# Sliding-window cached attention: K of the first unit as one load on ScalarE's queue, turned one projection chunk later; last output block in three pieces

## The chip, the cores and the metric

The kernel runs on one core of one Trainium2 chip. Its time is the device time of one execution in microseconds (us), and the figure for a kernel is the median of several executions. The engines have short names here: PE is TensorE (PEld its weight loads), DVE is VectorE, ACT is ScalarE, POOL is GpSimd, SP is SyncE. A DMA is started by an instruction on the queue of one engine, SP or ACT here, and carried out by 16 DMA engines. Inputs and output lie in device memory as bf16.

## The reference

```python
B, Sq, D = 8, 32, 1024;  Hq, Hkv, Sk, Dh = 32, 4, 8192, 128
W = min(4096, max(256, Sk // 4))          # 2048: the last 2048 keys
rep = Hq // Hkv                           # 8 query heads share a K/V head
q = (x @ wq) as (B, Hq, Sq, Dh)
k, v = the last W rows of the caches, repeated rep times
p = softmax(q k^T * Dh ** -0.5)
out = (p v) as (B, Sq, Hq * Dh) @ wo
```

The work is a query projection, attention of 256 query rows (8 heads by 32 positions) over 2048 keys for each of 32 units (8 sequences by 4 K/V heads), and an output projection.

## The kernel before, in words

The order of every engine is written by hand. `run` walks over the 32 units; a unit `ui` is (sequence b, group g), and units 0 to 7 are group 0. A unit has four chunks of four 128-key tiles. For each chunk PE computes the scores, keys on the partitions (L467), ACT takes the exponential without subtracting a maximum (L469), and two chunks later PE multiplies with V (L478). V is copied by DVE into a tile with a column of ones (L409), so that the last column of the result is the softmax sum; DVE divides by it (L415, L420) and turns the result for the output projection (L422). Queries of the next groups (L273) and the output projection (L293, gathered in the tile `oacc`) are spread over the chunks by a plan.

Scores need K with the head dimension on the partitions. Units 0 to 4 load K as it lies and turn it on PE, some later units turn it on DVE and POOL (L249, L257, L259), the others use a transposing DMA (L194). All loads go to SP's queue, except one half of x on ACT's. They are issued ahead of need, and DMAs share eight semaphores in turn, so that an issue waits until the semaphore's earlier DMA has landed.

`start` (L310) sets the order that matters here.
- **Loads.** x goes half to SP (L319), half to ACT (L320). Then on SP: the eight chunks of wq of group 0, as loads of 1, 1, 2, 2, 1 and 1 chunks with 2-KB rows (L162). K of unit 0 is loaded in two halves with 2-KB rows, one after wq chunks 4 and 5 (L324, issued at L191), one after chunk 7 (L327, issued at L186). Behind it come V of unit 0 and the K and V of units 1 to 3.
- **PE.** After seven warm-up matmuls (L345) PE turns x (L354). The copies out of PSUM go half to DVE and half to ACT (L357). Then come the eight chunks of the projection, eight matmuls each (L375). From chunk 4 on (`Q_CUT`) only the first 128 of 256 rows are done there. After chunk 5 (`c == self.DC - 3`) PE turns the first half of unit 0's K (L368, `k_turn(0)`), and DVE copies it to `kT` (L372, `k_copy(0)`). Chunks 6 and 7 follow, then the second half's turn.
- **After the loop.** The queries of unit 0 are cast out of four PSUM tiles, two by ACT and two by DVE (L395). After its two casts DVE copies the second half of K and then V of unit 0. The first scores need all four casts and the first half of K. The rest of the projection (`q_rest`) is placed between the first chunks of unit 0.

The end is in two functions. `tail_begin` finishes the last unit, counts on the device whether all softmax sums are in a safe range (`check_all`, L524 to L528), and starts the last output block: its first piece of 512 columns is multiplied ahead of a branch on that count (L76, L78). The branch leads to an exact fallback (`attention_exact`, `out_proj`), which the given inputs do not need. `tail_end` adds that piece to `oacc` (L303) and stores it (L305), then does the remaining pieces, of 256, 128 and 128 columns. The pieces share two PSUM buffers (`ps_m`). The stores of columns 0 and 768 go on SP's queue, the others on ACT's.

V of units 29 to 31 is loaded in two halves (`V_HALVES`, L200), all other V in one load.

Of the kernel before, what the change touches and what calls it, by code (L numbers as in the profile page):

```python
# [11 lines left out]
BF16 = mybir.dt.bfloat16  # L12
# [6 lines left out]
Q_CUT = 4  # L19
N_WARM = (7, 0, 0)  # L20
VA_ROW = 160
V_HALVES = 29

PE_T = (0, 1, 2, 3, 4)

# [77 lines left out]
class Fast:  # L103
# [69 lines left out]
                                   in_=self.wo[r0:r0 + 4 * self.Dh, :].rearrange("(p c) n -> p c n", c=4)[:, 2 * i:2 * i + 2, :])  # L173
        return [lambda i=i: piece(i) for i in range(2)]

    def load_k(self, ui, part=None):

        nc, P, KT = self.nc, self.P, self.KT
        b, g = self.units[ui]
        src = self.k_cache[b, g, self.Sk - self.W:, :]  # L180
        if ui not in V_T and ui not in self.kT:
            self.kT[ui] = self.ktp.tile([P, KT, P], BF16, name="kT")
        if ui in PE_T or ui in V_T:
            H = KT // 2
            if part == 1:
                nc.sync.dma_start(out=self.k_raw[ui][:, H:, :], in_=src.rearrange("(p j) d -> p j d", j=KT)[:, H:, :])  # L186
                return
            self.k_raw[ui] = (self.kvt.tile([P, KT, self.Dh], BF16, name="k_raw", tag="kv") if ui < 2 else
                              self.krp.tile([P, KT, self.Dh], BF16, name="k_raw"))
            n = KT if part is None else H  # L190
            nc.sync.dma_start(out=self.k_raw[ui][:, 0:n, :], in_=src.rearrange("(p j) d -> p j d", j=KT)[:, 0:n, :])  # L191
        else:
            H = KT // 2
            nc.sync.dma_start_transpose(out=self.kT[ui][:, part * H:(part + 1) * H, :],  # L194
                                        in_=src.rearrange("(p j) d -> p (j d)", j=KT)[:, part * H * P:(part + 1) * H * P])

    def load_v(self, ui, eng):
        b, g = self.units[ui]
        self.v_sb[ui] = self.vp.tile([self.P, self.KT, self.Dh], BF16, name="v_sb", tag="v")
        n = self.KT // (2 if ui >= V_HALVES else 1)  # L200
        for j in range(0, self.KT, n):
            eng.dma_start(out=self.v_sb[ui][:, j:j + n, :],
                          in_=self.v_cache[b, g, self.Sk - self.W:, :].rearrange("(p j) d -> p j d", j=self.KT)[:, j:j + n, :])

    def load_unit(self, ui):

# [73 lines left out]
    def o_pieces(self, g, t, cuts=(512, 512)):  # L280

        nc, P = self.nc, self.P
        st = {}
        last = g == self.Hkv - 1

        def piece(n0, w, i, mm=None):

            if i == 0:
                st["ps"] = self.open_ps = self.ps_m.tile([P, 512], FP32, name="op_ps", tag="m")
            ps = st["ps"]  # L290
            for k in range(i * 2, i * 2 + 2) if mm is not False else ():
                gq, c = g * self.QT_N + k // 4, k % 4
                nc.tensor.matmul(ps[:, 0:w], lhsT=self.OT[:, gq, c, t * P:(t + 1) * P],  # L293
                                 rhs=self.wo_t[gq][:, c, n0:n0 + w], start=(k == 0), stop=(k == 7))
            if i == 3 and mm is not True:
                acc = self.oacc[:, t, n0:n0 + w]
                if g == 0:
                    nc.vector.tensor_copy(out=acc, in_=ps[:, 0:w])
                elif not last:
                    nc.vector.tensor_tensor(out=acc, in0=ps[:, 0:w], in1=acc, op=ALU.add)  # L300
                else:
                    o_t = self.osb.tile([P, 512], BF16, name="o_t")
                    nc.vector.tensor_tensor(out=o_t[:, 0:w], in0=ps[:, 0:w], in1=acc, op=ALU.add)  # L303
                    eng = nc.sync if n0 in (0, 768) else nc.scalar
                    eng.dma_start(out=self.out[t * P:(t + 1) * P, n0:n0 + w], in_=o_t[:, 0:w])  # L305
        return [lambda n0=sum(cuts[:k]), w=w, i=i, **kw: piece(n0, w, i, **kw) for k, w in enumerate(cuts) for i in range(4)]

# [2 lines left out]
    def start(self):  # L310
        nc, P = self.nc, self.P
# [9 lines left out]
        wq0 = self.load_wq(0, 0, (1, 1, 2)) + self.load_wq(0, 1, (2, 1, 1))  # L321
        for p in wq0[:4]:
            p()
        self.load_k(0, 0)  # L324
        wq0[4]()
        wq0[5]()
        self.load_k(0, 1)  # L327
        self.load_v(0, nc.sync)
        self.load_k(1)
        self.load_v(1, nc.sync)  # L330
# [18 lines left out]
        def x_turn(half, pl, tag):  # L349
            ps = pl.tile([P, H, self.NT, P], BF16, name="xT_ps", tag=tag)  # L350
            for c in range(H):
                for t in range(self.NT):
                    c0 = (half * H + c) * P
                    nc.tensor.transpose(ps[:, c, t, :], x_sb[:, t, c0:c0 + P], self.ident[:, :])  # L354
            for i, copy in ((0, nc.vector.tensor_copy), (1, nc.scalar.copy)):
                c0 = half * H + i * H // 2
                copy(out=self.xT[:, c0:c0 + H // 2, :], in_=ps[:, i * H // 2:(i + 1) * H // 2, :, :].rearrange("p c t s -> p c (t s)"))  # L357

        x_turn(0, self.ps_m, "m")
        x_turn(1, self.ps_s, "s_ps")  # L360
        qs = [pl.tile([P, 2, self.NQ], FP32, name="q0_ps", tag=tag)
              for pl, tag in ((self.ps_o, "o_ps"), (self.ps_o, "o_ps"), (self.ps_m, "m"), (self.ps_m, "m"))]
        KT = self.KT
# [15 lines left out]
        for c in range(self.DC):  # L379
            for h in range(self.rep):  # L380
                q_mm(c, h, 0, P if c >= Q_CUT else self.NQ)
            if c == 0:
                warm_up(N_WARM[2])
                warm_sb = self.c1.tile([P, 8], BF16, name="warm_sb")
                nc.vector.tensor_copy(out=warm_sb[:, :], in_=warm[:, 0:8])
            if c == self.DC - 3:
                tp = self.ps_s.tile([P, KT, P], BF16, name="kf_ps", tag="s_ps")
                k_turn(0)
                k_copy(0)
# [105 lines left out]
    def tail_begin(self):  # L495
        self.pv_last()
        for p in self.after[:-2]:
            p()
        flagi = self.check_all()
        for p in self.after[-2:]:  # L500
            p()
        self.last = self.o_pieces(self.Hkv - 1, 1, (512, 256, 128, 128))
        for p in self.last[:3]:
            p()
        self.last[3](mm=True)
        return flagi
# [25 lines left out]
def attention_exact(tc, k_cache, v_cache, Q_e, OT_e, *, B, Hkv, Hq, Sq, Sk, W, Dh, scale):  # L532

    nc = tc.nc
# [5 lines left out]
    with ExitStack() as ctx:  # L540
# [12 lines left out]
        with tc.For_i(0, Hkv, 1) as g, tc.For_i(0, B, 1) as b:  # L553
# [27 lines left out]
            o_ps = ps_o.tile([P, UQ], FP32, name="o_ps")  # L581
            for j in range(KT):
                nc.tensor.matmul(o_ps[:, :], lhsT=v_sb[:, j, :], rhs=pT[:, j, :], start=(j == 0), stop=(j == KT - 1))
            nc.vector.tensor_copy(out=OT_e[:, :].rearrange("p (g h b s) -> p g h b s", g=Hkv, h=rep, b=B)[:, bass.ds(g, 1), :, bass.ds(b, 1), :],
                                  in_=o_ps[:, :].rearrange("p (g h b s) -> p g h b s", g=1, h=rep, b=1))


def out_proj(tc, wo, OT_e, out_flat, fast, *, Hkv, Hq, Sq, NQ, D):

    nc = tc.nc  # L590
    P = 128
    NT = NQ // P
    NC_ = D // 512
    rep = Hq // Hkv
    UQ = rep * Sq
    B = NQ // Sq
    with ExitStack() as ctx:
        wop = ctx.enter_context(tc.tile_pool(name="wo_pool", bufs=1))
        accp = ctx.enter_context(tc.tile_pool(name="acc_pool", bufs=1))
        pc = ctx.enter_context(tc.tile_pool(name="pc", bufs=1, space=PSUM))  # L600
        wo_v = wo.rearrange("(h p) n -> h p n", p=P)
        acc = accp.tile([P, NT, D], FP32, name="acc")
        nc.vector.memset(acc[:, :, :], 0.0)
        with tc.For_i(0, Hq, 1) as h:
            wo_sb = wop.tile([P, D], BF16, name="wo_sb")
            nc.sync.dma_start(out=wo_sb[:, :], in_=wo_v[bass.ds(h, 1), :, :].rearrange("o p n -> p (o n)"))
            o_h = wop.tile([P, NQ], BF16, name="o_h")
            nc.vector.tensor_copy(out=o_h[:, :], in_=OT_e[:, bass.ds(h * NQ, NQ)])
            ps = pc.tile([P, NT, D], FP32, name="ps")
            for t in range(NT):  # L610
                for n in range(NC_):
                    nc.tensor.matmul(ps[:, t, n * 512:(n + 1) * 512], lhsT=o_h[:, t * P:(t + 1) * P],
                                     rhs=wo_sb[:, n * 512:(n + 1) * 512], start=True, stop=True)
            nc.vector.tensor_tensor(out=acc[:, :, :], in0=ps[:, :, :], in1=acc[:, :, :], op=ALU.add)
        o_t = accp.tile([P, NT, D], BF16, name="o_t")
        nc.vector.tensor_copy(out=o_t[:, :, :], in_=acc[:, :, :])
        nc.sync.dma_start(out=out_flat.rearrange("(t p) d -> p t d", t=NT), in_=o_t[:, :, :])

        nc.vector.tensor_copy(out=fast.oacc[:, :, :], in_=acc[:, :, :])
        nc.vector.memset(fast.OT[:, (Hkv - 1) * fast.QT_N:, :, :], 0.0)  # L620
        nc.vector.memset(fast.open_ps[:, :], 0.0)
# [30 lines left out]
```

## Time and profile before

| What | us |
|---|---|
| Median of three runs (186.3 to 187.19) | 186.85 |
| The profiled execution, its own time | 186.85 |
| Span of its profile, first to last instruction | 185.0 |
| First score matmul of unit 0 | 13.32 |
| The last 128 output columns: addition begins | 182.34 |
| ACT busy, in all | 131.8 |
| DVE busy, in all | 115.4 |
| Mean rate of all DMA traffic | 280 GB/s |

The span is cut into 40 slices of 4.6 us. Each digit is the busy share of an engine in a slice, in tenths (9 is 90% or more). PEclk is PE's granted clock in tenths of full speed, DMA the mean busy share of the DMA engines, and the last row what they moved in GB/s:

```profile
PE   7999999999999999999999999999999999999993
DVE  0138799994586685586467558647745855355372
ACT  2207899786789787878787677787877888888700
PEclk9999999999999999999999999999999999999999
DMA  5999999998999999999999999999999999980012
GB/s 151 324 391 415 413 414 396 198 231 278 346 332 297 305 329 337 412 215 244 363 357 244 362 386 252 186 342 397 249 381 320 228 288 246 299 131 0 4 58 62
```

A reader can see three parts: a start of about three slices in which ACT and DVE have little to do, a long middle, and a short end in which the loads are over. In a timeline a line gives start, duration, engine, source line and operation, output and input names, the number of instructions, and in square brackets the idle time before them with what ended it. An engine name with a q (SPq, ACTq) is the engine's instruction queue, on which DMAs are issued.

### The profile page before, as it was taken

To read this page: it belongs to the slowest core of one execution; us is meant where nothing else is said; L and a number is where in the kernel's file an instruction comes from. 1 tells how busy PE (TensorE), PEld (TensorE's weight loads), DVE (VectorE), ACT (ScalarE), POOL (GpSimd) and SP (SyncE) were. 2 spreads that over 40 slices of the span, in tenths; PEclk is the share of its full clock that TensorE was granted. 3 is DMA by queue.
4 is the path that set the end of the run, shared out by engine and by line. 5 is a ranking of instruction groups with operands and counts; after the bars stand their busy time and mean duration, and the time that the engine had idled before them with its cause. 6 is when DMAs were issued, how large, how long until landed. Compare 5 with 4: busy or idle time off the path is not lost. (4 is left out here: it accounts for less than half of the span.)

```text
span 185.0 us, 5079 instructions
## 1 busy us (share of the span) xinstructions
PE 179.5 (97%) x2056; PEld 153.7 (83%) x2072; DVE 115.4 (62%) x268; ACT 131.8 (71%) x133; POOL 94.7 (51%) x150
## 2 busy tenths in 40 slices
PE   7999999999999999999999999999999999999993
PEld 2889999999999999987878999987777888888743
DVE  0138799994586685586467558647745855355372
ACT  2207899786789787878787677787877888888700
POOL 2000008949939959929944980796299289600000
PEclk9999999999999999999999999999999999999999
DMA  5999999998999999999999999999999999980012
GB/s 151 324 391 415 413 414 396 198 231 278 346 332 297 305 329 337 412 215 244 363 357 244 362 386 252 186 342 397 249 381 320 228 288 246 299 131 0 4 58 62
DMA packets 53082, 51.73 MB, mean 280 GB/s; under 512 B 39744, under 2 KB 40256, under 8 KB 53056
## 3 DMA queue, kind: packets, MB, share of 16 engines
q1 hardware_dynamic: 52480, 50.90, 97.8%
q10 hardware_dynamic: 576, 0.49, 0.8%
q8 instruction: 16, 0.26, 0.6%
q14 instruction: 10, 0.08, 0.1%
HBM read 41.42 MB, written 0.52 MB: 227 GB/s over the span
## 5 line engine op out<-in xcount | busy, mean ns | idle before, releaser
L469 ACT ACTIVATE pT<-s_ps 128x1024 bf16<-128x1024 f32 x128 | 128.9, 1025 | 33.3 <-PE s_ps L467 32.3
L259 POOL TENSOR_SCALAR kTv<-kb 32x512 bf16<-32x512 bf16 x140 | 93.7, 670 | 65.1 <-DMA k_raw<-in_k_cache_dram 26.7
L478 PEld LDWEIGHTS <-pT 128*128 128x128 bf16 x1024 | 68.5, 98 | 3.1
L467 PEld LDWEIGHTS <-kT 128*128 128x128 bf16 x368 | 34.8, 98 | 10.3
L293 PE MATMUL op_ps<-wo_sb,OT 128*128 128x512 bf16 (+2 forms) x128 | 33.0, 353 | 0.8
L273 PE MATMUL q_ps<-xT,wq_sb 128*128 128x256 bf16 x192 | 28.1, 273 | 0.0
L478 PE MATMUL o_ps<-va_112,pT 128*128 128x129 bf16 x352 | 27.1, 220 | 0.0
L478 PE MATMUL o_ps<-va_113,pT 128*128 128x129 bf16 x352 | 27.0, 220 | 0.1
L478 PE MATMUL o_ps<-va_114,pT 128*128 128x129 bf16 x320 | 24.7, 220 | 0.0
L249 DVE STREAM_TRANSPOSE kb<-k_raw 128x512 bf16<-128x512 bf16 x36 | 23.8, 684 | 0.0
L415 DVE RECIPROCAL RL_all<-o_ps 128x2 f32<-128x2 f32 x32 | 5.3, 164 | 27.5 <-PE o_ps L478 27.5
L420 DVE TENSOR_SCALAR o_sb<-o_ps,RL_all 128x128 bf16<-128x128 f32 x64 | 19.5, 346 | 1.1
L467 PEld LDWEIGHTS <-kTv 128*128 128x128 bf16 x144 | 13.9, 98 | 5.1
L273 PEld LDWEIGHTS <-wq_sb 128*128 128x128 bf16 x192 | 17.0, 98 | 1.2
L467 PE MATMUL s_ps<-QT_63,kT 128*128 128x256 bf16 x112 | 16.8, 273 | 0.0
L422 DVE STREAM_TRANSPOSE OT<-o_sb 128x256 bf16<-128x256 bf16 x32 | 14.3, 446 | 1.1
L467 PE MATMUL s_ps<-QT_66,kT 128*128 128x256 bf16 x96 | 14.4, 273 | 0.1
L293 PEld LDWEIGHTS <-OT 128*128 128x128 bf16 x144 | 11.3, 98 | 2.9 <-DVEq L78 0.6
L467 PE MATMUL s_ps<-QT_65,kT 128*128 128x256 bf16 x80 | 12.0, 273 | 0.1
L467 PE MATMUL s_ps<-QT_64,kT 128*128 128x256 bf16 x80 | 12.0, 272 | 0.1
L300 DVE TENSOR_TENSOR oacc<-op_ps,oacc 128x512 f32<-128x512 f32 x8 | 5.5, 683 | 7.4 <-PE op_ps L293 7.4
L409 DVE COPY va_113<-v_sb 128x2048 bf16<-128x2048 bf16 x11 | 9.5, 861 | 0.0
(46 smaller groups left out, 105.2 us busy)
## 6 DMA issues: line engine op xcount, KB each, us to landing
v_sb<-in_v_cache_dram SPq DMA_DIRECT2D x29, 512.0 KB, 6.8
wo_sb<-in_wo_dram SPq DMA_DIRECT2D x16, 512.0 KB, 6.8
wq_sb<-in_wq_dram SPq DMA_DIRECT2D x14, 512.0 KB, 7.4
k_raw<-in_k_cache_dram SPq DMA_DIRECT2D x13, 512.0 KB, 6.5
v_sb<-in_v_cache_dram SPq DMA_DIRECT2D x6, 256.0 KB, 5.8
wq_sb<-in_wq_dram SPq DMA_DIRECT2D x4, 256.0 KB, 6.4
kT<-in_k_cache_dram SPq DMA_TRANSPOSE x36, 6.6
k_raw<-in_k_cache_dram SPq DMA_DIRECT2D x2, 256.0 KB, 7.7
```

Of the source, the lines that this page charges most:

```text
L249: nc.vector.transpose(out=st["kb"][:, sl, :], in_=self.k_raw[ui][:, sl, :])
L259: nc.gpsimd.tensor_scalar(out=out, in0=in_, scalar1=1.0, scalar2=1.0, op0=ALU.mult, op1=ALU.mult)
L273: nc.tensor.matmul(st["ps"][:, 0:self.NQ], lhsT=self.wq_t[g, i][:, c % (DC // 2), hl * P:(hl + 1) * P], rhs=self.xT[:, c, :], start=(c == ...
L293: nc.tensor.matmul(ps[:, 0:w], lhsT=self.OT[:, gq, c, t * P:(t + 1) * P], rhs=self.wo_t[gq][:, c, n0:n0 + w], start=(k == 0), stop=(k == 7))
L300: nc.vector.tensor_tensor(out=acc, in0=ps[:, 0:w], in1=acc, op=ALU.add)
L409: self.nc.vector.tensor_copy(out=self.va[ui % 3][:, :, 0:self.Dh], in_=self.v_sb[ui][:, :, :])
L415: nc.vector.reciprocal(out=rl[:, ui * QT_N:(ui + 1) * QT_N], in_=o_ps[:, :, Dh])
L420: nc.vector.tensor_scalar(out=o_sb[:, qt, :, :], in0=o_ps[:, qt, 0:Dh].rearrange("p (i c) -> p c i", c=4), scalar1=rl[:, ui * QT_N + qt:ui ...
L422: nc.vector.transpose(out=self.OT[:, g * QT_N:(g + 1) * QT_N, :, b * self.Sq:(b + 1) * self.Sq], in_=o_sb[:, :, :, :])
L467: nc.tensor.matmul(s_ps[:, jj, :], lhsT=self.kT[ui][:, c * CJ + jj, :], rhs=q_u, start=True, stop=True)
L469: nc.scalar.activation(out=pT[:, :, :], in_=s_ps[:, :, :], func=ACT.Exp, bias=0.0, scale=self.scale)
L478: nc.tensor.matmul(o_ps[:, qt, 0:self.VW], lhsT=pT[:, jj, qt * P:(qt + 1) * P], rhs=va[:, j, 0:self.VW], start=(j == 0 and qt == 0), stop= ...
```

## The change

K of unit 0 is no longer loaded in two halves on SP's queue. It is one load with 4-KB rows, issued on ACT's queue after ACT's two copies of x. The turn of its first half and DVE's copy of it stand after projection chunk 6 (`c == self.DC - 2`) and no longer after chunk 5; the second half's turn stays after chunk 7. The last output block is cut into 512, 256 and 256 columns, and both pieces of 256 are stored on ACT's queue. V is always one load. In the fallback the tile `OT_e` keeps its results in another order, and the output projection there loops over four groups and no longer over 32 heads.

```diff
-V_HALVES = 29
...
-    def load_k(self, ui, part=None):
+    def load_k(self, ui, part=None, eng=None):
...
         if ui in PE_T or ui in V_T:
-            H = KT // 2
-            if part == 1:
-                nc.sync.dma_start(out=self.k_raw[ui][:, H:, :], in_=src.rearrange("(p j) d -> p j d", j=KT)[:, H:, :])
-                return
             self.k_raw[ui] = (self.kvt.tile([P, KT, self.Dh], BF16, name="k_raw", tag="kv") if ui < 2 else
                               self.krp.tile([P, KT, self.Dh], BF16, name="k_raw"))
-            n = KT if part is None else H
-            nc.sync.dma_start(out=self.k_raw[ui][:, 0:n, :], in_=src.rearrange("(p j) d -> p j d", j=KT)[:, 0:n, :])
+            (eng or nc.sync).dma_start(out=self.k_raw[ui][:, :, :], in_=src.rearrange("(p j) d -> p j d", j=KT))
...
-        n = self.KT // (2 if ui >= V_HALVES else 1)
-        for j in range(0, self.KT, n):
-            eng.dma_start(out=self.v_sb[ui][:, j:j + n, :],
-                          in_=self.v_cache[b, g, self.Sk - self.W:, :].rearrange("(p j) d -> p j d", j=self.KT)[:, j:j + n, :])
+        eng.dma_start(out=self.v_sb[ui][:, :, :],
+                      in_=self.v_cache[b, g, self.Sk - self.W:, :].rearrange("(p j) d -> p j d", j=self.KT))
...
-                    eng = nc.sync if n0 in (0, 768) else nc.scalar
+                    eng = nc.sync if n0 == 0 else nc.scalar
...
         for p in wq0[:4]:
             p()
-        self.load_k(0, 0)
         wq0[4]()
         wq0[5]()
-        self.load_k(0, 1)
         self.load_v(0, nc.sync)
...
         x_turn(1, self.ps_s, "s_ps")
+        self.load_k(0, eng=nc.scalar)
...
-            if c == self.DC - 3:
+            if c == self.DC - 2:
                 tp = self.ps_s.tile([P, KT, P], BF16, name="kf_ps", tag="s_ps")
                 k_turn(0)
                 k_copy(0)
...
-        self.last = self.o_pieces(self.Hkv - 1, 1, (512, 256, 128, 128))
+        self.last = self.o_pieces(self.Hkv - 1, 1, (512, 256, 256))
...
-        with tc.For_i(0, Hq, 1) as h:
+        with tc.For_i(0, Hkv, 1) as g:
...
+            for h in range(rep):
+                for t in range(NT):
+                    for n in range(NC_):
+                        nc.tensor.matmul(ps[:, t, n * 512:(n + 1) * 512], lhsT=o_v[:, h, t * P:(t + 1) * P],
+                                         rhs=wo_sb[:, h, n * 512:(n + 1) * 512], start=(h == 0), stop=(h == rep - 1))
```

More of the change, by code (lines that the diff above doesn't have):

```diff
@@ L183, in load_k @@
         if ui in PE_T or ui in V_T:
-            H = KT // 2
-            if part == 1:
-                nc.sync.dma_start(out=self.k_raw[ui][:, H:, :], in_=src.rearrange("(p j) d -> p j d", j=KT)[:, H:, :])
-                return
             self.k_raw[ui] = (self.kvt.tile([P, KT, self.Dh], BF16, name="k_raw", tag="kv") if ui < 2 else
                               self.krp.tile([P, KT, self.Dh], BF16, name="k_raw"))
-            n = KT if part is None else H
-            nc.sync.dma_start(out=self.k_raw[ui][:, 0:n, :], in_=src.rearrange("(p j) d -> p j d", j=KT)[:, 0:n, :])
+            (eng or nc.sync).dma_start(out=self.k_raw[ui][:, :, :], in_=src.rearrange("(p j) d -> p j d", j=KT))
         else:
+            H = KT // 2
             H = KT // 2
@@ L583, in attention_exact @@
                 nc.tensor.matmul(o_ps[:, :], lhsT=v_sb[:, j, :], rhs=pT[:, j, :], start=(j == 0), stop=(j == KT - 1))
-            nc.vector.tensor_copy(out=OT_e[:, :].rearrange("p (g h b s) -> p g h b s", g=Hkv, h=rep, b=B)[:, bass.ds(g, 1), :, bass.ds(b, 1), :],
-                                  in_=o_ps[:, :].rearrange("p (g h b s) -> p g h b s", g=1, h=rep, b=1))
+            nc.vector.tensor_copy(out=OT_e[:, bass.ds(g * (B * UQ) + b * UQ, UQ)], in_=o_ps[:, :])
 def out_proj(tc, wo, OT_e, out_flat, fast, *, Hkv, Hq, Sq, NQ, D):
@@ L600, in out_proj @@
         pc = ctx.enter_context(tc.tile_pool(name="pc", bufs=1, space=PSUM))
-        wo_v = wo.rearrange("(h p) n -> h p n", p=P)
+        wo_v = wo.rearrange("(g h p) n -> g p h n", p=P, h=rep)
         acc = accp.tile([P, NT, D], FP32, name="acc")
         nc.vector.memset(acc[:, :, :], 0.0)
-        with tc.For_i(0, Hq, 1) as h:
[L605 to L608, printed above, removed]
-            ps = pc.tile([P, NT, D], FP32, name="ps")
[L610 to L613, printed above, removed]
+        with tc.For_i(0, Hkv, 1) as g:
+            wo_sb = wop.tile([P, rep, D], BF16, name="wo_sb")
+            nc.sync.dma_start(out=wo_sb[:, :, :], in_=wo_v[bass.ds(g, 1), :, :, :].rearrange("o p h n -> p (o h) n"))
+            o_g = wop.tile([P, rep, B, Sq], BF16, name="o_g")
+            nc.vector.tensor_copy(out=o_g[:, :, :, :].rearrange("p h b s -> p b h s"),
+                                  in_=OT_e[:, bass.ds(g * (B * UQ), B * UQ)].rearrange("p (b h s) -> p b h s", b=B, h=rep))
+            o_v = o_g[:, :, :, :].rearrange("p h b s -> p h (b s)")
+            ps = pc.tile([P, NT, D], FP32, name="ps")
+            for h in range(rep):
[3 more added lines that the diff above has]
+                                         rhs=wo_sb[:, h, n * 512:(n + 1) * 512], start=(h == 0), stop=(h == rep - 1))
             nc.vector.tensor_tensor(out=acc[:, :, :], in0=ps[:, :, :], in1=acc[:, :, :], op=ALU.add)
```

## The prediction

> **What bounds the kernel now.** I read the page's busy shares first, then the busy time by stretches, then the timelines of the two ends, because the change touches only the first 17 us and the last few.
>
> ```profile
> PE 179.5 (97%) x2056; PEld 153.7 (83%) x2072; DVE 115.4 (62%) x268; ACT 131.8 (71%) x133; POOL 94.7 (51%) x150
> 20.00:40.00 20.00, 20.00 (x273) 18.98 (x271) 18.78 (x41) 17.25 (x18) 8.41 (x13) 1.00 1.13 331
> 40.00:60.00 20.00, 20.00 (x250) 18.72 (x248) 13.02 (x35) 16.53 (x18) 15.66 (x24) 1.00 1.12 307
> ```
>
> TensorE is busy for 179.5 of 185.0 us. In the stretches (columns: stretch, length, then PE, PEld, DVE, ACT, POOL busy, clock, DMA share, GB/s) it has no idle time from 20 to 60 us, and the further stretches up to 176 us lose at most 0.21 us in each 20. So no slack later swallows a delay: if the first score matmul of unit 0 moves by some time, the end moves by the same. What counts is when that matmul starts (13.27 us now) and how long the tail is.
>
> The start, from the timeline (start, duration, engine, line):
>
> ```profile
> 6.03 1.19 ACT L357 COPY xT<-xT_ps 128x512 bf16<-128x512 bf16 x2 [3.57 <-DVE xT L357]
> 10.77 0.49 PEld L368 LDWEIGHTS <-k_raw 128*128 128x128 bf16 x8
> 11.47 0.69 DVE L372 COPY kT<-kf_ps 128x1024 bf16<-128x1024 bf16 x1 [4.80 <-PE kf_ps L368]
> 12.23 0.45 PEld L375 LDWEIGHTS <-wq_sb 128*128 128x128 bf16 x8 [0.38 <-DMA wq_sb<-in_wq_dram]
> 12.67 0.45 DVE L395 CAST QT_63<-q_ps 128x64 bf16<-128x64 f32 x2 [0.50 <-PE q_ps L375]
> 12.86 0.45 PEld L368 LDWEIGHTS <-k_raw 128*128 128x128 bf16 x8 [0.19 <-DMA k_raw<-in_k_cache_dram]
> 13.27 0.37 PEld L467 LDWEIGHTS <-kT 128*128 128x128 bf16 x4
> ```
>
> Chunk 7 of the projection (12.23) and the second half of K (12.86) each wait for a DMA. The start is paced by data arriving in SP's line: issue time plus time to landing gives wq chunks 4 and 5 at 9.8, K's first half 10.7, chunk 6 11.3, chunk 7 12.1, K's second half 12.85, V of unit 0 14.1. The four pieces of 256 KB in 2-KB rows from 9.8 to 12.85 took 0.765 us each; V, 512 KB in 4-KB rows, took 1.23 us. The first half's turn and its 0.69-us copy to kT are done at 12.16, while TensorE still waits for chunk 7.
>
> The tail:
>
> ```profile
> 180.15 1.05 PE op_ps L293 x8
> 181.22 0.43 DVE o_t L303
> 181.70 0.62 PE op_ps L293 x8
> 182.34 0.29 DVE o_t L303
> ```
>
> The chain that ended last: the 256-column piece, its addition, which frees the PSUM buffer, the last 128 columns, their addition to 182.63. Their store is issued at 182.66 and lands 1.5 us later.
>
> **The change, part by part.**
>
> 1. **The load of K moves to ACT's queue.** In ACT's order it stands behind the two xT copies, so it is issued at about 7.22 instead of 3.10 and 4.95. Its semaphore was used last by wq chunk 1, landed at about 6.8, so no wait is added there. Behind it ACT has only the QT casts, and ACT is idle until 12.55 (5.34 us for q_ps): an issue of some 0.4 us (0.40 for x_sb) is hidden, and would cost 0.4 if that cover were gone. SP loses two issues (0.47 and 0.48); chunks 6 and 7 are issued up to 0.95 earlier, yet they stand 7.6 us in line, so this buys nothing by itself.
> When does K land? The only row with both queues at work is x: two halves of 256 KB, issued together at 0.74, landed after 3.7 and 3.8 us. Taking off 2 x 0.765 leaves 2.2 us of fixed delay, so K's data flow from about 9.4. In 3.0 to 3.5 us SP's queue moved 52 packets and ACT's 49: even shares. From 9.8 the engines owe chunk 6 (0.765), chunk 7 (0.765) and K (1.23, as V): all three are there at 9.8 + 2.76 = 12.55, some 0.3 us sooner than now thanks to the 4-KB rows. Chunk 6 and K together cannot be there before 9.8 + 0.765 + 1.23 = 11.8.
>
> 2. **The turn of half 0 stands behind chunk 6.** If K lands first and chunk 6 at 11.8, the chunk's eight weight loads take 0.45 and the turn starts at 12.25; if K shares with chunk 7 and lands last, it starts at up to 12.55. I take the middle, 12.4. Behind the turn TensorE's order holds chunk 7, half 1's turn and the first score: 0.45 + 0.45 + 0.40, so TensorE itself would be ready 1.3 us later. DVE is later still, as its order is: copy of half 0, two QT casts, copy of half 1. In the trace the copy begins 0.70 after the turn's start (10.77 to 11.47); it takes 0.69, the casts 0.45, and the step to TensorE some 0.05: 1.89 in all. The copy that was hidden behind chunks 6 and 7 is now on the path. First score: 12.4 + 1.89 = 14.29, against 13.27: **+1.02 us**. Bounds: below, chunk 7 at 12.55 with the copy hidden; from its start to the score the trace has 1.04 (12.23 to 13.27), so 13.6, +0.35. Above, K waits in line as the first six loads of K on SP did, 7.6 to 10.6 us: 14.8 at the shortest, score 16.7, +3.4.
> Units 0 and 1 do not lose further: V of unit 0 comes at about 12.55 + 1.23 = 13.8 (14.1 now), and K of unit 1 landed at 15.4 for a use at 16.82, with the same bytes ahead of it. DVE's copy of V still ends 1.3 us after the first score, ahead of its use 3.0 us after it.
>
> 3. **Last block in 512, 256 and 256.** The second 256 piece takes the PSUM buffer that the addition of the 512 piece freed at 180.73, so TensorE runs on: eight matmuls at 0.12 spacing from about 181.1 end at 182.05, the addition (0.43 by the row) at 182.50 instead of 182.63: **-0.13 us**. The store is 64 KB rather than 32; both sizes landed in 1.5. If the larger store took the 1.7 of the 128-KB rows, the gain would be gone, +0.07.
>
> 4. **V of units 29 to 31 in one piece.** Their halves land at about 157.9, 160.1 and 163.5 and are copied at 161.90, 164.29 and 169.72: 4 us of cover. SP saves three issues at 0.5, off the path. Cost nothing; if the cover were gone, a whole load is 1.0 us later by the rows (6.8 against 5.8).
>
> 5. **The fallback's new loops** are not run. They lengthen TensorE's program behind the branch; the nearest row is the 0.61 us that TensorE now waits at the branch. Bounds -0.6 to +0.6; I take nothing, since both programs jump over the code.
>
> **Sum:** 1.02 - 0.13 = +0.89. The profiled execution took 186.85 us with its span of 185.0, and that is also the median of the three runs: 186.85 + 0.89 = **187.7 us**. Half a percent, about what a measurement can tell from no change here, is 0.93, so the forecast lies on the edge between no change and slower.
>
> **Two rules weighed.** The row has 0.765 us for 256 KB in 2-KB rows against 1.23 for 512 KB in 4-KB rows, a fifth less per byte. The Trainium skill (DMA: Bandwidth & Descriptors, section "Why a DMA increments its semaphore by 16 and not by 1") has 2 KiB per partition as enough to saturate the DMAs, which speaks against any gain from 4-KB rows; by it K would take 1.53, everything 0.3 later, and the sum would be 188.0. The measured rows decide. The same page (section "Queues, rings and completion order") lets an engine drain a whole packet of some 9 to 17 descriptors of one queue before it turns to another; K's 128 rows are 8 for each engine, so by it K would come in one turn, ahead of chunk 6, and the sum would be 187.6; the 52 to 49 packets of x are too coarse to show it.
>
> **The rivals.**
> - **ACT's queue is late (slower).** K misses the fair share, and the turn, with TensorE's whole order behind it, waits. For it: a 128-KB store on ACT's queue at 179.03 took 3.0 us to land, on SP's 1.7. Against it: x on ACT's queue took 3.8, on SP's 3.7. Fair sharing alone has K at 9.4 + 2 x 1.23 = 11.9; with the extra 1.3 it is 13.2, the score at 15.1, and the time 186.85 + 1.8 - 0.1 = 188.5; at the upper bound of +3.4 it is 190.1. It decides once K lands after 12.55.
> - **Two queues fill the DMA engines better (not slower).** For it: the rate dips to 250 and 277 GB/s from 8 to 10 us, with 416 to 430 from 12 to 14. If chunks 6 and 7 take 0.62 each, the rate of the later stretch, all is there at 9.8 + 1.24 + 1.23 = 12.27, the score follows chunk 7 at 13.3, and with the tail the time is 186.75. It needs K before 11.4 too, so that DVE's copy hides again. Against it: the engines' busy share was already 0.9 to 1.05 in the dip.
> - **The change does nothing at the start**, because data pace it either way: the lower bound +0.35, with the tail 187.1.
>
> **How the numbers follow.** Fair sharing, 187.7 with 187.1 to 188.0: 0.60 (nothing at the start is its lower edge). Late queue, 188.5 with up to 190.1: 0.25. Better filled: 0.12, 186.4 to 187.0. Something not seen: 0.03. Slower by over 0.5% (above 187.78) is nearly half of the first, 0.27, and the late queue, 0.25: 0.52. Within 0.5%: 0.33 and 0.11 from the first and third, 0.44. Faster: 0.04. The range 186.9 to 189.2 leaves out the lower half of the third case and the far end of the second.
>
> **What would show it.** In the changed profile: the load of K issued by ACT near 7.2 and landed 4 to 5.3 us later; the first turn at 12.25 to 12.55; DVE's first kT copy right before the QT casts with no gap; TensorE idle some 0.6 us ahead of the first score, which starts near 14.3; all later steps shifted by as much; the last addition 0.13 us nearer to the branch than now. Wrong would be a turn that starts before 11.5 or after 13, a first score back at 13.3, or a shift that shrinks along the run.

## The result and the profile after

The changed kernel takes 191.74 us (median of six runs, 190.79 to 192.13) against 186.65 (six runs, 186.3 to 187.19). The ratio is 1.026, with a 95% interval of 1.023 to 1.030. The profiled execution took 192.07 us, with a span of 190.3. The forecast was 187.7, the range 186.9 to 189.2: wrong, with the right sign.

The start in the timeline of the changed kernel (start, duration, engine, line):

```profile
7.39 0.34 ACTq L185 DMA_DIRECT2D k_raw<-in_k_cache_dram  x1
15.11 0.45 PEld L360 LDWEIGHTS <-k_raw 128*128 128x128 bf16 x8 [3.31 <-DMA k_raw<-in_k_cache_dram]
15.11 0.62 PE L360 MATMUL kf_ps<-ident,k_raw 128*128 128x128 bf16 x8 [3.14 <-DMA k_raw<-in_k_cache_dram]
15.77 0.69 DVE L364 COPY kT<-kf_ps 128x1024 bf16<-128x1024 bf16 x1 [9.22 <-PE kf_ps L360]
16.38 0.35 DVE L387 CAST QT_63<-q_ps 128x64 bf16<-128x64 f32 x2
17.21 0.68 PEld L459 LDWEIGHTS <-kT 128*128 128x128 bf16 x4
17.32 1.06 PE L459 MATMUL s_ps<-QT_63,kT 128*128 128x256 bf16 x4
19.54 0.37 PEld L459 LDWEIGHTS <-kT 128*128 128x128 bf16 x4
```

K is issued at 7.39 (7.22 was forecast) and lands 7.7 us later. TensorE, done with chunk 6, waits 3.1 us for it. The first score follows at 17.21 (13.27 before). The second is 4.94 later than before (19.54 against 14.60) and not 3.94. The reason stands in the busy time by stretches (the number behind the POOL column is the granted clock):

```profile
13.00:14.00 1.00, 0.00 (x0) 0.00 (x0) 0.00 (x0) 0.00 (x0) 0.00 (x0) 1.00 1.02 414
15.00:16.00 1.00, 0.89 (x15) 0.89 (x16) 0.23 (x1) 0.12 (x1) 0.00 (x0) 0.92 1.01 414
16.00:17.00 1.00, 0.85 (x9) 0.69 (x7) 0.72 (x3) 0.30 (x2) 0.00 (x0) 0.50 1.03 422
18.00:19.00 1.00, 1.00 (x10) 0.93 (x9) 0.85 (x2) 0.59 (x1) 0.00 (x0) 0.50 1.03 418
20.00:21.00 1.00, 1.00 (x19) 0.99 (x18) 0.83 (x2) 0.77 (x1) 0.00 (x0) 1.00 1.00 410
```

The clock is 1.00 during the wait and 0.50 from about 15.8, 0.7 us after TensorE works again, until about 19.3. The kernel before had 1.00 throughout.

When K moved is seen in the DMA view of the changed kernel, cut into half microseconds: 10.5 to 11 (first line), 11 to 11.5 (next two), 12.5 to 13 (last two). The columns are packets, MB, and share of the 16 engines; q1 is SP's queue, q10 ACT's.

```profile
q1 hardware_dynamic: 44, 0.16, 91.8%
q1 hardware_dynamic: 43, 0.14, 74.4%
q10 hardware_dynamic: 17, 0.07, 33.8%
q1 hardware_dynamic: 29, 0.12, 57.6%
q10 hardware_dynamic: 24, 0.10, 47.7%
```

K's first data come at 11.0, 3.6 us after the issue. From 12 to 13.5 the two queues have about half each (25 to 29 packets of q1 beside 24 to 28 of q10); before and after, K has less. K's last data move at about 14.4, and it has landed at 15.1.

The end, in the chain that ended last:

```profile
185.08 1.92 PE op_ps L286 x16
187.00 0.02 issue
187.03 0.42 DVE o_t L296
```

The two pieces of 256 run through without the stop for the buffer. The last addition ends at 187.45 and the span at 190.3, 2.85 us later; before it was 182.63 and 185.0, 2.37.

**The account** of the 5.3 us between the spans: first score matmul 4.00 later (13.32 to 17.32); from there to the last addition 170.13 against 169.31, which is 0.94 more with a slow clock and 0.12 less in the tail (169.19 in the profiles below that have the new tail, the full clock and no new wait); after the last addition 0.48. That makes 4.00 + 0.94 - 0.12 + 0.48 = 5.30, so no other wait grew along the run.

### The profile page after: what moved, and what is told of

Its sections match the earlier page's. It is cut to its first block, busy times and chain, and to the rows that moved or that the text cites. A ratio compares the mean times of both kernels' runs of the same rounds, so it can differ in the third digit from the quotient of the medians.

```text
span 190.3 us, 5052 instructions
## 1 busy us (share of the span) xinstructions
PE 180.7 (95%) x2048; PEld 154.8 (81%) x2064; DVE 115.2 (61%) x267; ACT 131.8 (69%) x133; POOL 94.7 (50%) x150
## 5 line engine op out<-in xcount | busy, mean ns | idle before, releaser
L286 PE MATMUL op_ps<-wo_sb,OT 128*128 128x512 bf16 (+1 forms) x120 | 32.9, 365 | 0.8
L412 DVE TENSOR_SCALAR o_sb<-o_ps,RL_all 128x128 bf16<-128x128 f32 x64 | 19.5, 347 | 1.1
L459 PE MATMUL s_ps<-QT_66,kT 128*128 128x256 bf16 x96 | 14.4, 273 | 0.1
```

The source lines that it names most:

```text
L412: nc.vector.tensor_scalar(out=o_sb[:, qt, :, :], in0=o_ps[:, qt, 0:Dh].rearrange("p (i c) -> p c i", c=4), scalar1=rl[:, ui * QT_N + qt:ui ...
L459: nc.tensor.matmul(s_ps[:, jj, :], lhsT=self.kT[ui][:, c * CJ + jj, :], rhs=q_u, start=True, stop=True)
```

## The experiments

A line of three dots marks code that is left out. Two questions had to be told apart: which part of the change costs the time, and why K is late. The theory was that K is late because it enters the DMA engines late and beside a full line, and that the wait slows the clock; the rivals were that ACT's queue is slow in itself, that the other parts cost the time, or that DVE's copy does.

**Everything but the K part.** The changed kernel with K's loads and turn as before:

```diff
...
+        self.load_k(0, 0)
         wq0[4]()
         wq0[5]()
+        self.load_k(0, 1)
...
-        self.load_k(0, eng=nc.scalar)
...
-            if c == self.DC - 2:
+            if c == self.DC - 3:
```

> All of the change but its K part: K of unit 0 is loaded and turned as before; last block in 512, 256, 256, V whole, the fallback's new loops. The profile of the changed kernel puts the loss at its start, so this should come out with the time of before: 186.5, within 0.3. Prediction's terms: -0.13 for the tail, nothing for V and the fallback. Rival, a late last store: in the changed kernel 2.85 us pass from the last addition to the end of the span, 2.37 before, so +0.35 and 187.0.

187.48 against 186.95, ratio 1.0026 (1.0011 to 1.0041): 0.5 us, more than the 0.3 that was allowed for and near the rival's figure. From the last addition (183.24) to the end of the span (186.1) it was 2.86. The rest of the change is not free, but it is a tenth of the loss.

**Only the turn moved.** The kernel before with one line changed:

```diff
-            if c == self.DC - 3:
+            if c == self.DC - 2:
```

> The kernel before with the turn of K's first half moved behind chunk 6 and nothing else; K comes as before. By the prediction's term for DVE's copy: the turn starts at 11.8, the copy ends 1.39 later and the casts at 13.6, first score at 13.66 against 13.27, +0.4 us, 187.05. Rival, the copy stays hidden behind chunk 7: no change, 186.65.

187.29 against 186.95, ratio 1.0016 (1.0007 to 1.0025), so +0.3 where 0.4 was expected. Its timeline on TensorE and DVE:

```profile
12.35 0.61 PE L368 MATMUL kf_ps<-ident,k_raw 128*128 128x128 bf16 x8
13.00 0.69 DVE L372 COPY kT<-kf_ps 128x1024 bf16<-128x1024 bf16 x1 [6.39 <-PE kf_ps L368]
13.74 0.61 PE L368 MATMUL kf_ps<-ident,k_raw 128*128 128x128 bf16 x8 [0.34 <-DVE kT L372]
14.19 0.60 PE L467 MATMUL s_ps<-QT,kT 128*128 128x256 bf16 x4
```

From the turn to the first score it is 1.84 us; the prediction had 1.89 by way of the casts. The way is another one: half 1's turn writes the same PSUM tile that the copy of half 0 is reading, and TensorE waits for that copy (0.34). The two ways cost the same here.

**K on SP's queue.** The changed kernel, with the one load of K put into SP's line:

```diff
             p()
+        self.load_k(0)
         wq0[4]()
...
-        self.load_k(0, eng=nc.scalar)
```

> The changed kernel with K's one load in 4-KB rows put on SP's queue behind wq chunks 4 and 5, the turn behind chunk 6. Theory that the late issue on ACT's queue is the cause: K is there at about 11, ahead of chunk 6, first score near 13.9, total about 187.2. Rival, one whole load or its place behind chunk 6 is the cause: first score later than 16, total above 190.

188.26, ratio 1.0079 (1.0056 to 1.0102). The median is 1.3 over before. In the profiled execution (187.90 us, a span of 186.1, 1.1 over before) the first score is at 14.06 and the clock 1.00: the first score has 0.74 (14.06 - 13.32), the tail -0.12, and 0.48 more pass after the last addition (2.85). Not all of the 0.74 need be the change's: kernels that load and turn K as before have first scores from 13.2 to 14.05. So the size of K's load and its place behind chunk 6 are not what cost 5 us: the queue and the moment are.

**K early on ACT's queue.**

```diff
         nc.scalar.dma_start(out=x_sb[:, 1, :], in_=xf[P:2 * P, :])
+        self.load_k(0, eng=nc.scalar)
...
-        self.load_k(0, eng=nc.scalar)
```

> The changed kernel with K's load issued on ACT's queue right behind x, near 1.2 us and not 7.4. Theory that K is late because it is issued behind the xT copies into engines that SP's line keeps busy: K lands by 7 us, the weights come later by at most K's own 1.2 us, first score near 13.9, total about 187.2. Rival, a load on ACT's queue is slow in itself: it lands 7.7 us after its issue or later, so near 9, which the turn at 12 still does not feel; the landing tells the two apart, not the total.

189.82, ratio 1.0158 (1.0142 to 1.0174): the total missed by 2.6. K landed 6.8 us after its issue, at 8.0, between the two forecasts. A new loss came: the first weights came at 7.5, TensorE waited 1.9 us, and the clock was 0.50 from 8.0 to 11.4:

```profile
4.00:5.00 1.00, 0.88 (x8) 0.45 (x8) 0.00 (x0) 0.00 (x0) 0.00 (x0) 1.00 0.77 143
6.00:7.00 1.00, 0.00 (x0) 0.00 (x0) 0.20 (x2) 0.79 (x2) 0.00 (x0) 1.00 0.90 320
9.00:10.00 1.00, 1.00 (x7) 0.72 (x5) 0.00 (x0) 0.00 (x0) 0.00 (x0) 0.50 1.05 408
```

The low rate from 4 to 6 us (143 and 201 GB/s) is not what is new: the kernel with everything but the K part has 111 and 221 there, the kernel before 262 and 381. Why the rate dips at all stays open. New is who gets it. From 4 to 7 us K moved 0.45 MB on ACT's queue (q10), and SP's queue (q1), with the weights, only 0.23; in the kernel with everything but the K part SP's queue moved 0.65. The half microsecond from 6 to 6.5:

```profile
q10 hardware_dynamic: 28, 0.11, 60.3%
q1 hardware_dynamic: 18, 0.02, 24.6%
```

So an earlier issue does not make the move free: K then takes the engines from the weights, which TensorE needs first.

**TensorE kept busy.** 56 more transposes of the identity, ahead of the turn:

```diff
+N_FILL = 56
...
+                for i in range(N_FILL):
+                    nc.tensor.transpose(tp[:, i % KT, :], self.ident[:, :], self.ident[:, :])
                 k_turn(0)
```

> The changed kernel with 56 more transposes of the identity ahead of the turn of K's first half, into places that the turn writes anew: 56 at 0.056 us keep TensorE busy for the 3.1 us in which it waits for K. Theory that the wait makes the granted clock fall to 0.5 from 16 to 19 us, which costs 1.0 on top of the late K: clock 1.00 throughout, 190.7. Rival, these steps are slow for another reason, as DVE or the loads: still 191.7.

190.55 (190.51 to 190.61), ratio 1.0196 (1.0179 to 1.0213). In the profile K lands at 14.1 (6.8 us after its issue at 7.34; 15.1 in the changed kernel), and the turn begins when the transposes let it:

```profile
11.72 3.29 PE L382 MATMUL kf_ps<-ident 128*128 128x128 bf16 x56
14.85 0.61 PE L361 MATMUL kf_ps<-ident,k_raw 128*128 128x128 bf16 x8
```

The stretches behind it read:

```profile
15.00:16.00 1.00, 0.91 (x17) 0.79 (x15) 0.50 (x1) 0.38 (x2) 0.00 (x0) 1.00 1.02 410
16.00:17.00 1.00, 0.76 (x11) 0.73 (x11) 0.57 (x4) 0.05 (x1) 0.00 (x0) 1.00 0.96 389
```

The clock stays at 1.00; the mean clock is 1.00 in all four executions, and 0.99 in all six of the changed kernel. The time is 1.2 us below the changed kernel's 191.74, of which 0.26 is the earlier turn. Between the two profiles the turn takes 1.84 us to the first score and not 2.21, and from there to the last addition it is 169.19 and not 170.13: 1.31 in all. So the slow clock is the work of the wait, and it costs 1.0 to 1.3 us.

**SP's line held until K has landed.**

```diff
         wq0[5]()
-        self.load_v(0, nc.sync)
-        self.load_k(1)
-        self.load_v(1, nc.sync)
...
         self.load_k(0, eng=nc.scalar)
...
+        nc.scalar.copy(out=self.v_sb[0][:, 0, 0:8], in_=self.k_raw[0][:, self.KT - 1, 0:8])
+        self.load_v(0, nc.sync)
+        self.load_k(1)
+        self.load_v(1, nc.sync)
...
```

> The changed kernel, but SP's loads behind the weights (V of unit 0, K of unit 1 and all later ones) are not issued until K of unit 0 has landed; an 8-column copy on ACT, which V's load overwrites, makes them wait. Theory that K is late because it shares the DMA engines half and half with loads issued before it: first data near 10.5, landed by 12.5, first score near 14.5. V of unit 0 then lands near 16.5 and still in time, total about 188.5. Rival, ACT's queue is slow under its own power: K lands near 15 again, total above 191.

189.73, ratio 1.0141 (1.0118 to 1.0164). K was issued at 6.57, its first data came between 9.5 and 10 (some 3.2 us later), and it had landed when ACT's copy ran:

```profile
12.74 0.20 ACT L350 COPY v_sb<-k_raw 128x8 bf16<-128x8 bf16 x1 [5.59 <-DMA k_raw<-in_k_cache_dram]
14.61 0.60 PE L462 MATMUL s_ps<-QT,kT 128*128 128x256 bf16 x4
17.39 0.69 DVE L404 COPY va<-v_sb 128x2048 bf16<-128x2048 bf16 x1 [1.89 <-DMA v_sb<-in_v_cache_dram]
18.67 0.61 PE L473 MATMUL o_ps<-va,pT 128*128 128x129 bf16 x8 [0.80 <-DVE QT L390]
```

The first score is where the theory had it, and K landed after 6.1 us instead of 7.7. But 3.2 us of that pass before any data, and the rest is not all the work of sharing. K's data, from the first packet to the last, took 2.5 us here and 3.4 in the changed kernel; with the line as full as there they took 2.5 (TensorE kept busy) and 2.6 (the K part alone, below), and K landed after 6.8 in both. So the larger part of the delay is the wait for the first data. What sharing with the loads behind the weights adds differs from run to run, and why the first data wait so long stays open.

The total is 1.2 us worse than expected because V of unit 0 now came late: DVE's copy of V waited 1.89 us for it, DVE's casts stand behind that copy, and the first matmul with V waited 0.80 for them. From the first score to the last addition it is 170.40 us, 1.21 over the 169.19.

**The tail alone**, with the last store on ACT's queue, and again on SP's. The first line pair is in both kernels, the second in the first kernel only:

```diff
-        self.last = self.o_pieces(self.Hkv - 1, 1, (512, 256, 128, 128))
+        self.last = self.o_pieces(self.Hkv - 1, 1, (512, 256, 256))
...
-                    eng = nc.sync if n0 in (0, 768) else nc.scalar
+                    eng = nc.sync if n0 == 0 else nc.scalar
```

> The kernel before with the last block in 512, 256, 256 and the last two stores on ACT's queue, nothing else. If the tail is what cost 0.5 us where all but the K part was changed: 187.3 to 187.5, and some 2.85 us from the last addition to the end of the span instead of 2.4. Rival, V of the last units or the fallback's code cost it: 186.8, the prediction's -0.13.

> The same three pieces, but the store of the last 256 columns on SP's queue, as the kernel before has it for columns from 768 on. If the cost is two stores one after the other on ACT's queue: back to 2.4 us after the last addition, and 186.8. Rival, the size of the last store (64 KB against 32) costs it: 187.3 as with both on ACT's queue.

186.92 and 186.98 against 186.97; ratios 1.0000 (0.9990 to 1.0011) and 1.0005 (0.9994 to 1.0016). First score to last addition is 169.19 in both, 0.12 less than before, the prediction's -0.13; the end after it is 2.47 and 2.52 instead of 2.37 and takes most of the gain back. A tenth is near what one profile can tell, as the next runs show, and the totals tell no gain and no loss. The queue of the last store makes no measurable difference.

**The fallback's code alone, and V whole alone** (`V_HALVES = 99`):

> The kernel before with the fallback's new loops and nothing else; that code is not run. The run of all but the K part was 0.49 us slower than before, the tail alone 0.0, so V of the last units or the fallback's code has the 0.5. If it is the code: 187.4, with output stores that land late at the end. Rival, the code costs nothing, as the prediction took it: 186.95.

> The kernel before with V of units 29 to 31 in one load each and nothing else. The prediction has 4 us of cover and so no change: 186.95. Rival, it has the 0.5 that the run of all but the K part lost: 187.4, and then one of the last copies of V would wait for its load.

187.11 and 187.23 against 187.09; ratios 1.0002 (0.9994 to 1.0011) and 1.0011 (1.0001 to 1.0020). So the code that is not run costs nothing by itself, and V some 0.2, at most 0.4. The tail, the fallback and V together make 0.25 where all of them in one kernel cost 0.49 (0.21 to 0.77): the intervals meet. A hint of more is in the stores of the profiles. The two lines are the output store of 128 KB on ACT's queue, of the tail alone and of the fallback alone:

```profile
out_dram<-o_t ACTq DMA_DIRECT2D x1, 128.0 KB, 2.7
```

```profile
out_dram<-o_t ACTq DMA_DIRECT2D x1, 128.0 KB, 4.0
```

In the six profiles with the new fallback and the new tail this store lands 3.4 to 4.2 us after its issue, in those with the old fallback 2.7 to 3.3. Those six, which all have V whole too, have 2.82 to 2.92 from the last addition to the end of the span. The fallback alone has 2.37, as before, V whole alone 2.59, the tail alone 2.47 and 2.52. Why all three together make it longer was not settled.

**The K part alone**, on the kernel before:

> The kernel before with the K part alone: one load in 4-KB rows on ACT's queue after the xT copies, turn behind chunk 6. If the parts add up: the changed kernel's 5.1 us less the 0.5 of the rest, so 191.5 here; K lands 6.8 to 7.7 us after its issue, the turn starts near 15, the clock falls. Rival, the parts need each other (fewer DMA semaphores in use, another layout): 189 or less.

190.68 (189.56 to 191.42), ratio 1.0175 (1.0149 to 1.0201): +3.6. The turn began at 14.85, the clock fell to 0.50, the first score was at 17.27. With the 0.5 of the rest it makes 4.1 of 5.1: the K part is most of the loss, below the 191.5 that was expected, and 1.0 is left over. The four executions differ by up to 1.9. The lowest, 189.56, has a mean clock of 1.00, the other three 0.99, so there the clock did not fall. The profiled one, at 191.42, is the slowest of the four, with a TensorE wait of 2.3 us.

**A load on ACT's queue in mid-stream.** V of unit 3, on the kernel before:

```diff
-            self.load_v(ui, self.nc.sync)
+            if ui != 3:
+                self.load_v(ui, self.nc.sync)
...
+                if ui == 0 and c == 1:
+                    self.load_v(3, nc.scalar)
```

> The kernel before with V of unit 3 (512 KB, 4-KB rows) issued on ACT's queue behind the second exponential, near 16.5 us, while SP's line is full of 4-KB rows; needed near 29. In the changed kernel K's first data came 3.6 us after its issue, and 1.37 MB of SP's line moved in between, about 40 packets for each engine. If an engine first finishes a number of packets that SP's line has already given it: some 38 packets of 4 KB, 2.4 MB, so first data 5 to 6 us after the issue. Rival, a fixed delay of a busy machine: 3.2 to 3.6 us again. The total is 186.9 to 187.3 either way.

187.15 against 187.09, ratio 1.0005 (0.9994 to 1.0016). Issued at 15.57; the DMA view from 18.5 to 19 (first line), 19 to 19.5, and its landing:

```profile
q1 hardware_dynamic: 57, 0.21, 102.0%
q1 hardware_dynamic: 39, 0.13, 64.4%
q10 hardware_dynamic: 20, 0.08, 39.8%
v_sb<-in_v_cache_dram ACTq DMA_DIRECT2D x1, 512.0 KB, 7.2
```

First data about 3.5 us after the issue: the rival's fixed 3.2 to 3.6, not the 5 to 6 of a fixed number of packets. My idea that an engine first works off some 38 packets falls.

## Why the prediction was wrong

- **The step that failed** is "Taking off 2 x 0.765 leaves 2.2 us of fixed delay, so K's data flow from about 9.4". The delay was taken from x, issued into empty engines. Beside a full line 3.2 to 3.7 us pass before the first data alone (five profiles), data flowed from 11.0, and at half rate or less K landed at 15.1. The turn began at 15.11 and not at 12.4: 2.7 us, of which 1.6 lie ahead of the first data and 1.1 behind it. With it fell the sum "all three are there at 12.55": chunks 6 and 7 landed at 10.5 and 12.1, so K came behind nearly all of them and shared with V of unit 0 and K of unit 1.
- **A term that was missing.** The prediction let TensorE wait and asked nothing of its clock. A wait of 3.1 us halved it, which cost 0.37 up to the first score (2.21 us from the turn, 1.84 at the full clock) and 0.94 behind it.
- **The bounds.** "14.8 at the shortest" for the turn was near the truth, but I gave this case 0.25, and the range left out its far end. Without the clock's term even that end, 190.1, was too low.
- **Right: the copy on the path.** 1.84 measured where 1.89 was worked out, though the wait is TensorE's for the copy, not the casts' turn on DVE. The move of the turn costs 0.3 alone, and 0.4 was its expectation.
- **Right in size, wrong in effect: the tail.** -0.12 up to the last addition, forecast -0.13. In the changed kernel 0.48 more after the last addition outweighs it; with the tail alone no gain is left in the total. The prediction followed the last store only to "both sizes landed in 1.5".
- **Right: no slack.** The 4.9 us at the second score were still 4.8 at the last addition.
- **V whole and the fallback** were put at nothing. Alone they measure 0.2 and 0.0; the 0.49 of all three other parts is more than forecast and not wholly explained.
- **The even shares** of two queues held in the main: 25 to 29 packets beside 24 to 28 from 12 to 13.5 with K, and near even with x. The Trainium skill (DMA: Bandwidth & Descriptors, section "Queues, rings and completion order") has an engine drain a packet of some 9 to 17 descriptors before it turns to another queue. By that K, 8 rows for each engine, should have come in one turn, if a row is one descriptor. These runs speak against it: in the profile K makes 144 packets, 128 rows of 4 KB and 16 short ones that come last, as many as there are engines. None of the short ones came before 13.0, 2 us after the first data. Eight rows at one go would take 1.23 us by the row of V.

- **The gain of 4-KB rows** is smaller than the fifth that was taken. In the changed kernel the weights' 2-KB rows moved at 385 GB/s from 9 to 9.5 us, and the 4-KB rows behind them at 418 from 12 to 20. The prediction's 0.765 us for 256 KB, 343 GB/s, holds the low rates from 8 to 10 us (250 and 277), so it is no price of the row size alone.

## What to carry to other kernels

A load on another engine's queue does not jump the line: beside a full queue, count a start-up delay measured beside a full queue, then half the rate, then the slowest of the engines. A transfer that TensorE waits for belongs into the one line, in the order of use, if its issue on the other queue comes later than it would in the line. When a wait on TensorE grows to microseconds (1.9 was enough here, 1.2 was not), price the clock as well as the wait.

## What the runs showed of the hardware

- A load on ACT's queue beside a busy SP queue: first data 3.2 (held line), 3.5 (K part alone and V of unit 3), 3.6 (changed kernel) and 3.7 us (TensorE kept busy) after the issue, with 2-KB or 4-KB rows ahead. Beside nearly empty engines 1.3 to 2.1 us (x: issued at 0.74, first packets of ACT's queue between 2.0 and 2.9). 512 KB landed 6.1 to 7.7 us after the issue.
- The granted clock fell to 0.50 after a TensorE wait of 3.1 us (changed kernel), 2.3 (K part alone) and 1.9 (K early), not in the wait but 0.3 to 0.7 us after the work began again, and stayed there for 3.4 us in all three; after a wait of 1.2 (held line) it stayed at 1.00. The Trainium skill (TensorE: Matmul & The Clock Gate, section "HAM oscillation — how this bites in real kernels") sets the limit at idle gaps of about 3.4 us; here 1.9 and 2.3 were enough.
- The start of the same loads varies: kernels that load and turn K as before had their first score matmul between 13.2 and 14.05 us, with a dip of the DMA rate at 4 to 6 us of varying depth (111 to 262 GB/s from 4 to 5).
